# Merging small table and tail transfers, moving one decay to VectorE and two copies to ScalarE in a retention and two-MoE kernel

## The chip, the cores and the metric

One core of a Trainium2 chip runs the whole kernel. The metric is device time in microseconds, the median of several runs; one more execution is profiled and gives the trace. TensorE is called PE in the rows, VectorE DVE, ScalarE ACT, GpSimd POOL and SyncE SP. The cores' engines run side by side, each taking its own instructions in order, and wait for each other by semaphores.

## The reference

Three layers follow each other, in float32. `gamma` is one decay per head.

```
q, k, v: [4 batches, 8 heads, 576 tokens, 64]
scores = q @ k.T / 8 ;  ret = scores * gamma**(i - j) where i >= j, else 0
x = (ret @ v), heads side by side             -> [2304 tokens, 512]
h = x @ w_in ; g = h * sigmoid(1.702 h) ; x = g @ w_out          (2048 wide)
expert = argmax of cosine(x, expert_emb) / tau over 8 experts, gate = its softmax
out = gate * (relu(x @ w1[expert]) @ w2[expert])                 (1024 wide)
```

## The kernel before

The work is laid out by hand: every engine's instructions are emitted in a fixed order, and a float32 product is made of three products of a high and a low part. Four stages follow each other: attention (to about 71 us), the dense layers with the router beside them, the experts, and the last results. The change touches attention alone.

Attention works on "rows". A row is one batch and one pair of heads, so there are 16: rows 0 to 3 are batch 0, rows 4 to 7 batch 1, and so on. The first 512 of the 576 tokens are four chunks of 128; the 64 left over are the "ends" or "tails". A row comes in one transfer of 1024 KB (8 KB on each of 128 partitions): transposed keys, transposed queries, keys and values. The tails of a batch are a separate tensor, 768 bytes on each partition for each of four pairs. The decay tables are a third, 572 bytes on each partition and pair, after two masks that all pairs share. `load(bp)` issues the transfers that go with row `bp`, nearly all from SP's one queue, in the order in which they are called. Rows 0 to 8 are called for at the start, rows 9 to 15 when the slot of an earlier row is free. SP holds back an issue until the transfer eight issues earlier has landed, and PE's, VectorE's or GpSimd's reading of a slot when the slot is taken again.

Rows are computed in groups: [0], [1, 2], [3, 4], ... [13, 14], [15]. For a group `rows` with `nxt` and `then` the next two, the loop emits, in this order: GpSimd's decays for `then` (`decay_ends` scales the tails' queries of batches 2 and 3, `decay` the keys of a row, `decay_queries` the queries of batches 2 and 3); on PE the part of the output that comes from earlier chunks (`carried`) and the ends (`ends_out`), then `scores_end(nxt)`, the end products of the next group, then `scores` of the first row of `nxt`; on VectorE `masks` of that row (two instructions); then `values`, which interleaves on PE the chunks of `rows` with the four states of `nxt`. `state` multiplies decayed keys and values on PE, and ScalarE scales the result (L357). PE takes its instructions in order, so a late input of one holds up those behind it.

`DVE_ROWS` lists the rows whose `decay` VectorE does; all others are GpSimd's. For batches 0 and 1 an output row leaves PSUM by VectorE's multiplication (`keep`, L413). For batches 2 and 3 `keep` lets VectorE copy the odd rows (L409), and `kept_out` lets ScalarE copy those that are left (L419). The outputs have two banks of PSUM in turn, so row 15 takes the one that row 13 left.

From the group with row 11 on, a generator (`convert`) fills VectorE and ScalarE with the unpacking of the dense layers' weights: magnitude (ScalarE, L168), clamp and shift (VectorE, L181 and L183), two insertions (L191 and L196), high part (ScalarE, L171), low part (VectorE, L175). `flush` emits the pending magnitude or high part at the `yield`s. The dense layers begin with `layer1` (L576), the gate (ScalarE's tanh at L607, VectorE's product at L609) and `layer2` (L587).

Of the kernel before, what the change touches and what calls it, by code (L numbers as in the profile page):

```python
# [19 lines left out]
NPAIR = H // 2  # L20
# [26 lines left out]
STOP = 1000.0  # L47
EARLY = 5
WD_AT = (EARLY, 8, 9)
DVE_ROWS = (0, 2, 7, 8, 9)  # L50
NWD = 3
NBUF = 9
NBP = B * NPAIR
# [24 lines left out]
def retention_moe_kernel(  # L78
# [161 lines left out]
    def attention_(psum):  # L240
# [19 lines left out]
        def load(bp):  # L260
            t = row[bp]
            b, pair = divmod(bp, NPAIR)

            def load_tab(lo, hi):
                lo, hi = TX * (lo > 0) + TW * lo, TX + TW * hi
                SP.dma_start(tb[:, lo:hi], tab[:, lo:hi])

            def load_tails(lo, hi):
                SP.dma_start(tl[b][:, lo:hi], tails[b, :, lo:hi])

            if bp == 0:
                SP.dma_start(t[:, :AK], att[bp, :, :AK])
                ACT.dma_start(t[:, AK:], att[bp, :, AK:])
                load_tab(0, 1)
            if pair == 0:
                load_tails(0, 1 if b < 2 else NPAIR)
            if bp == 2:
                SP.dma_start(t[:, AK:], att[bp, :, AK:])
                load_tails(1, NPAIR)
                SP.dma_start(t[:, :AK], att[bp, :, :AK])  # L280
            elif bp:
                SP.dma_start(t, att[bp])
            if bp == 1:
                load_tab(1, 3)
            if bp == 2:
                load_tab(3, 4)
            if bp == 4:
                load_tails(1, NPAIR)

        load(0)  # L290
        DVE.memset(ones, 1.0)
# [11 lines left out]
        for bp in range(1, NBUF):  # L303
            load(bp)
# [19 lines left out]
        def masks(bp):  # L324
            pr = prs[bp % 3]
            for j in range(2):
                y, sc = (a.rearrange("p (c q) -> p c q", q=P) for a in (pr[:, 512 * j : 512 * (j + 1)], scs[j]))
                g = tbs[:, bp % NPAIR, TM + j : TM + j + 1]
                DVE.scalar_tensor_tensor(y, sc, g, tri.unsqueeze(1).to_broadcast(y.shape), ALU.mult, ALU.mult)  # L329

        def decay(bp):
            if bp < NBP:
                kd = row[bp][:, AK:AV].rearrange("p (c e) -> p c e", e=HD)
                dec = tbs[:, bp % NPAIR, TK:TS]
                (DVE if bp in DVE_ROWS else POOL).tensor_tensor(kd, kd, dec.unsqueeze(2).to_broadcast(kd.shape), ALU.mult)

        def decay_ends(bp):
            b, pair = divmod(bp, NPAIR)
            if b > 1 and pair == 0:
                qe = tl[b][:, :, TQ:TV]  # L340
                POOL.tensor_tensor(qe, qe, tbs[:, :, :TAIL], ALU.mult)

        def decay_queries(bp):
            b, pair = divmod(bp, NPAIR)
            if b > 1:
                qd = row[bp][:, AQ:AK].rearrange("p (c q) -> p c q", q=P)
                POOL.tensor_tensor(qd, qd, tbs[:, pair, :P].unsqueeze(1).to_broadcast(qd.shape), ALU.mult)

        def state(bp, ch):
            t = row[bp]  # L350
            if ch == 0:
                st["kv", bp] = psum.tile([P, 64], F32, tag="kv", bufs=2, name=f"s{bp}")
            s = st["kv", bp]
            for j, r in enumerate(heads):
                c0 = P * ch + 64 * j
                PE.matmul(s[r], t[:, AK + c0 : AK + c0 + 64], t[:, AV + c0 : AV + c0 + 64], start=ch == 0, stop=True, skip_group_check=ch > 0)  # L356
            ACT.activation(kvs[bp % 2][:, 64 * ch : 64 * ch + 64], s, AF.Copy, scale=tbs[:, bp % NPAIR, TS + ch : TS + ch + 1])  # L357
# [5 lines left out]
        def carried(bp):  # L363
            t, kv = row[bp], kvs[bp % 2]
            new_out(bp)
            for ch in range(1, NCH):
                for r in heads:
                    o = st["o", bp][r, P * ch : P * (ch + 1)]
                    first = ch == 1 and bp > 0
                    PE.matmul(o, kv[r, 64 * (ch - 1) : 64 * ch], t[r, AQ + P * ch : AQ + P * (ch + 1)], start=first, stop=True, skip_group_check=not first)  # L370
# [11 lines left out]
        def chunk(bp, ch):  # L382
            t, pr = row[bp], prs[bp % 3]
            for j, r in enumerate(heads):
                o = st["o", bp][r, P * ch : P * (ch + 1)]
                c0 = AV + P * ch + 64 * j
                first = bp + ch == 0
                PE.matmul(o, t[:, c0 : c0 + 64], pr[:, 512 * j + P * ch : 512 * j + P * (ch + 1)], start=first, stop=True, skip_group_check=not first)  # L388

        def kept_in(bp):  # L390
            b, pair = divmod(bp, NPAIR)
            if b > 1:
                tok = b * S - 2 * TB
                return x0f[pair][:, tok : tok + S]
            if ("x", bp) not in st:
                st["x", bp] = pool.tile([P, S], F32, tag="row", bufs=6, name=f"x{bp}")
            return st["x", bp]
# [7 lines left out]

        def keep(bp):
            if bp // NPAIR > 1:
                if bp % 2:
                    DVE.tensor_copy(kept_in(bp)[:, : NCH * P], st.pop(("o", bp)))  # L409
                return  # L410
            x, dec = kept_in(bp), tbs[:, bp % NPAIR, :P]
            y, o = (a.rearrange("p (c q) -> p c q", q=P) for a in (x[:, : NCH * P], st["o", bp]))
            DVE.tensor_tensor(y, o, dec.unsqueeze(1).to_broadcast(y.shape), ALU.mult)  # L413
# [26 lines left out]
        def values(rows, nxt):  # L440
            out = [(bp, ch) for bp in rows for ch in range(NCH)]
            at = [0, 3, 6, 8]
            for k, (bp, ch) in enumerate(out + [(None, None)]):
                if k in at and len(rows) + len(nxt) > 1:
                    for r in nxt:
                        state(r, at.index(k))
                if bp is not None:
                    chunk(bp, ch)
                if ch == NCH - 1:
                    keep(bp)  # L450
# [15 lines left out]
        for k, rows in enumerate(groups):  # L466
            nxt, then = (groups + [[], []])[k + 1 : k + 3]
            for bp in then:
                decay_ends(bp)
            for bp in then:  # L470
                if bp > 2 and bp not in DVE_ROWS:
                    decay(bp)
                decay_queries(bp)
            for bp in rows:
                carried(bp)
            ends_out(rows)
            if k:
                scores_end(nxt)
            for bp in rows:
                keep_end(bp)  # L480
            if k > 5:
                yield False
            if nxt:
                scores(nxt[0])
            if k == 0:
                decay(2)
                masks(nxt[0])
                keep(0)
                for ch in range(NCH):
                    for bp in nxt:  # L490
                        state(bp, ch)
                    if ch == 1:
                        scores(nxt[1])
                        masks(nxt[1])
                    else:
                        idle(4)
                scores_end(nxt)
            else:
                if nxt:
                    masks(nxt[0])  # L500
                values(rows, nxt)
            for bp in rows:
                if ("o", bp) in st:
                    kept_out(bp)
            make_lows(0 if k < 6 else 1)
            for bp in rows:
                if bp in WD_AT:
                    load_wd(WD_AT.index(bp))
                if bp in follows:
                    load(follows[bp])  # L510
                if follows.get(bp) == NBP - 1:

                    st["loaded"] = True
                    SP.dma_start(c[:, :CET], cst[:, :CET])
                    SP.dma_start(c[:, CET : CET + KD * E], embt)
                    uf = pool.tile([P, P], F32, tag="cvb", bufs=1, name="uf")
                    SP.dma_start(uf, cst[:, CU:CSL])
                    load_due()
            if k > 5:
                yield True  # L520
            for bp in nxt[1:] if k else []:
                scores(bp)
                masks(bp)
            for bp in then:
                if bp > 2 and bp in DVE_ROWS:
                    decay(bp)
            if 4 < k < 8:
                yield True
# [856 lines left out]
```

## Time and profile before

| | |
|---|---|
| median of 3 runs | 720.91 us (718.78 to 721.19) |
| profiled execution, its own time | 719.96 us |
| its span, first to last instruction | 718.1 us |
| PE busy | 702.8 us (98%) |
| PE weight load busy | 653.3 us (91%) |
| VectorE busy | 453.3 us (63%) |
| ScalarE busy | 306.6 us (43%) |
| GpSimd busy | 204.9 us (29%) |
| mean granted clock of TensorE | 0.995 of full speed |

The busy times are sums over the span. Matmuls are pipelined and their ends are modelled, so a row of PE can overlap the next one by some tenths of a microsecond, and a busy PE may hold short waits. The granted clock is the share of TensorE's full speed that the throttle let through.

### The profile page before, as it was taken

What the parts mean: (1) busy time and instruction counts of PE and PEld (TensorE: products, weight loads), DVE (VectorE), ACT (ScalarE), POOL (GpSimd) and SP (SyncE); (2) the same over time, 40 slices, a digit from 0 to 9 for tenths busy, and PEclk for the clock granted to TensorE, in tenths of its full rate; (3) what the DMA queues carried; (4) which work ended last, traced back from release to release, by engine and by line L of the source; (5) the groups of instructions that cost most, each with busy time, mean ns of one, the idle gap of its engine ahead of it and who ended that gap; (6) DMA issues with size and microseconds to landing.
All of it is one profiled execution on the core that took longest, in us unless ns stands there. A gap on an engine that the chain in (4) does not pass through costs nothing.

```text
span 718.1 us, 13166 instructions
## 1 busy us (share of the span) xinstructions
PE 702.8 (98%) x4903; PEld 653.3 (91%) x4903; DVE 453.3 (63%) x1036; ACT 306.6 (43%) x598; POOL 204.9 (29%) x193
## 2 busy tenths in 40 slices
PE   9999999999999999999999999999999999999995
PEld 7899789999989998998999899989999999998994
DVE  4678898888338886764475478555664464563551
ACT  3345454454273333322332253353454554554542
POOL 0773000000000240300120112323445656555563
PEclk9999999999999999999999999999999999999998
DMA  8999999000310040200300412235497979989761
GB/s 334 415 410 333 397 336 302 2 1 1 136 44 1 1 132 1 89 0 15 119 1 0 147 34 84 81 111 150 170 272 219 281 214 245 233 264 246 246 186 62
DMA packets 53156, 113.41 MB, mean 158 GB/s; under 512 B 8146, under 2 KB 29138, under 8 KB 48992
## 3 DMA queue, kind: packets, MB, share of 16 engines
q1 hardware_dynamic: 49744, 102.55, 44.8%
q0 software_dynamic: 3200, 9.46, 3.9%
q8 instruction: 39, 0.64, 0.4%
q10 hardware_dynamic: 144, 0.52, 0.2%
q14 instruction: 29, 0.24, 0.1%
HBM read 84.67 MB, written 28.17 MB: 157 GB/s over the span
## 4 chain that ended last, share of the span: by engine, by line
PE 82%; DMA 8%; DVE 3%; issue 3%; SPq 2%; ACT 1%; POOL 1%; POOLq 0%; ACTq 0%; DVEq 0%
PE o L587 28%; PE h L576 27%; PE eh L576 10%; PE eo L597 9%; DMA row<-att 3%; DMA we<-we 2%; PE ao L388 2%; PE sc L313 2%; DMA yd<-yq 1%; DMA y<-yd 1%; PE ao L370 1%; PE s L356 1%; SPq L836 1%; ACT unit L220 1%; DVE unit L221 1%
## 5 line engine op out<-in xcount | busy, mean ns | idle before, releaser
L576 PE MATMUL h<-x,unit 128*128 128x384 f32 x1152 | 217.5, 337 | 0.6 <-DVE g0t L609 0.6
L576 PEld LDWEIGHTS h<-x,unit 128*128 128x128 f32 x1152 | 204.6, 188 | 9.2 <-DVE g0t L609 0.9
L222 POOL TENSOR_TENSOR unit<-we,unit 128x512 fp32r<-128x512 f32 x64 | 103.1, 1619 | 120.8 <-ACT unit L220 102.8
L576 PE MATMUL eh<-xt,unit 128*128 128x336 f32 (+6 forms) x672 | 102.2, 301 | 0.7 <-DVE eg48l L621 0.6
L576 PEld LDWEIGHTS eh<-xt,unit 128*128 128x128 f32 x672 | 95.4, 188 | 1.5 <-DVE eg48l L621 0.8
L221 DVE TENSOR_TENSOR unit<-we,unit 128x512 fp32r<-128x512 f32 x64 | 53.6, 838 | 62.6 <-ACT unit L220 58.6
L220 ACT CAST unit<-we 128x1024 fp32r<-128x1024 f32 x64 | 66.8, 1046 | 26.9 <-DMA we<-we 24.7
L683 DVE CUSTOM_DVE_ANT_0 dj<-xr,en 128x512 bf16<-128x512 f32 x120 | 78.1, 698 | 0.0
L649 POOL TENSOR_TENSOR enrm<-scr,c 128x8 f32<-128x8 f32 x1 | 1.7, 1688 | 153.5 <-ACT ej L654 153.5
L626 POOL DMA_INDIRECT out<-y,idx x24 | 24.1, 1004 | 29.5 <-ACT y L849 19.2
L357 ACT ACTIVATE ends<-s,tb 128x64 f32<-128x64 f32 x64 | 17.4, 312 | 32.6 <-PE s L356 29.6
L626 POOL DMA_INDIRECT xs<-xr,slot x18 | 19.4, 1078 | 39.1 <-DVE xr L758 35.7
L743 POOL TENSOR_TENSOR cum<-cum,oh_all 128x8 bf16<-128x8 bf16 x18 | 4.8, 268 | 67.1 <-PE rk L736 52.4
L175 DVE TENSOR_TENSOR unit<-ca,unit 128x1024 fp32r<-128x1024 f32 x16 | 19.5, 1221 | 3.1 <-ACT unit L171 3.1
L549 POOL TENSOR_TENSOR x<-x0s,x 128x768 fp32r<-128x768 f32 x3 | 6.1, 2032 | 48.6 <-ACT x L548 48.6
L191 DVE SCALAR_TENSOR_TENSOR ca<-wd,ca 128x1024 int32<-128x1024 int32 x16 | 19.6, 1222 | 0.3
L196 DVE SCALAR_TENSOR_TENSOR ca<-wd,ca 128x1024 int32<-128x1024 int32 x16 | 19.5, 1219 | 0.1
L329 DVE SCALAR_TENSOR_TENSOR pr<-sc,tb 128x512 f32<-128x512 f32 x22 | 15.5, 745 | 5.9 <-PE sc L313 5.9
L849 ACT ACTIVATE y<-y,gate 128x512 f32<-128x512 f32 (+7 forms) x21 | 14.3, 713 | 11.1 <-DMA y<-yd 9.6
L313 PE MATMUL sc<-row 64*128 64x128 f32 x256 | 18.6, 285 | 0.3
L817 ACT CAST xt<-tp 128x336 fp32r<-128x336 f32 (+6 forms) x28 | 11.1, 411 | 18.2 <-DVE tp L815 18.2
L168 ACT ACTIVATE ca<-wd 128x1024 f32<-128x1024 f32 x16 | 18.4, 1152 | 0.0
(1311 smaller groups left out, 1531.7 us busy)
## 6 DMA issues: line engine op xcount, KB each, us to landing
we<-we SPq DMA_DIRECT2D x64, 512.0 KB
wd<-wd SPq DMA_DIRECT2D x16, 1024.0 KB
row<-att SPq DMA_DIRECT2D x14, 1024.0 KB
xs<-fill SPq DMA_DIRECT2D x22, 257.0 KB
xrow<-xr SPq DMA_DIRECT2D x18, 257.0 KB
y<-yd SPq DMA_DIRECT2D x7, 512.0 KB
x0d<-x0f SPq DMA_DIRECT2D x4, 768.0 KB
x0s<-x0d SPq DMA_DIRECT2D x8, 384.0 KB
```

The source lines that it names most:

```text
L175: DVE.tensor_tensor(units[u][:, 1, :], word(u).bitcast(F32), units[u][:, 0, :].bitcast(F32), ALU.subtract)
L191: DVE.scalar_tensor_tensor(a, d[:, :, 1], -0x40000000, a, ALU.bitwise_and, ALU.bitwise_or)
L196: DVE.scalar_tensor_tensor(a, d[:, :, 0], 29, a, ALU.logical_shift_right, ALU.bitwise_or)
L220: ACT.copy(w[:, 0, :], t)
L221: DVE.tensor_tensor(w[:, 1, :512], t[:, :512], w[:, 0, :512].bitcast(F32), ALU.subtract)
L222: POOL.tensor_tensor(w[:, 1, 512:], t[:, 512:], w[:, 0, 512:].bitcast(F32), ALU.subtract)
L313: PE.matmul(scs[j][:, P * ch : P * (ch + 1)], t[r, P * ch : P * (ch + 1)], t[r, AQ + P * ch : AQ + P * (ch + 1)], start=True, stop=True)
L576: PE.matmul(h, w[:, a, P * dc : P * (dc + 1)], xt[:, b, dc, :n], start=k == 0, stop=k == len(terms) - 1)
L587: PE.matmul(o, a[:, c0 : c0 + n], w[:, b, 512:], start=first and k == 0, stop=last and k == 2)
L597: PE.matmul(o, w[:, b, D + P * d : D + P * (d + 1)], a, start=first and k == 0, stop=last and k == 2)
L626: i = POOL.indirect_dma_start(out=dst[:, :], out_offset=bass.IndirectOffsetOnAxis(ap=rows, axis=0), in_=src, in_offset=None, bounds_check= ...
L683: DVE.tensor_tensor_reduce(junk, r[:, :D], en[e // 4][:, e % 4, :], 1.0, 0.0, ALU.mult, ALU.add, dots[:, E * k + e : E * k + e + 1])
```

## The change

Four things change, all in attention. The tables of pairs 1 to 3 come in one transfer instead of two (pairs 1 and 2, then 3). The tails of batch 1 come in one transfer, issued behind row 4, instead of one pair ahead of row 4 and three behind it; the tails of batches 2 and 3, which were one transfer each already, are issued behind the first row of their batch instead of ahead of it. VectorE decays row 4; its instruction stands in group [1, 2] behind the masks of row 3. VectorE no longer copies the outputs of rows 13 and 15, so `kept_out` has ScalarE copy them.

```diff
-DVE_ROWS = (0, 2, 7, 8, 9)
+DVE_ROWS = (0, 2, 4, 7, 8, 9)
...
-            if pair == 0:
-                load_tails(0, 1 if b < 2 else NPAIR)
+            if bp == 0:
+                load_tails(0, 1)
             if bp == 2:
                 SP.dma_start(t[:, AK:], att[bp, :, AK:])
                 load_tails(1, NPAIR)
                 SP.dma_start(t[:, :AK], att[bp, :, :AK])
             elif bp:
                 SP.dma_start(t, att[bp])
+            if b and pair == 0:
+                load_tails(0, NPAIR)
             if bp == 1:
-                load_tab(1, 3)
-            if bp == 2:
-                load_tab(3, 4)
-            if bp == 4:
-                load_tails(1, NPAIR)
+                load_tab(1, NPAIR)
...
         def keep(bp):
             if bp // NPAIR > 1:
-                if bp % 2:
+                if bp % 2 and bp < NBP - 3:
                     DVE.tensor_copy(kept_in(bp)[:, : NCH * P], st.pop(("o", bp)))
                 return
...
                 if nxt:
                     masks(nxt[0])
+                if k == 1:
+                    decay(4)
                 values(rows, nxt)
...
             for bp in then:
-                if bp > 2 and bp in DVE_ROWS:
+                if bp > 4 and bp in DVE_ROWS:
                     decay(bp)
```

## Rows read from the trace of the kernel before

**Rows 1.** Windows: stretch, its us, busy us (instructions) by engine, clock, DMA share, GB/s.
```profile
22.00:66.00 44.00, 44.00 (x858) 40.75 (x854) 31.78 (x56) 22.55 (x74) 30.20 (x32) 1.00 0.98 388
...
70.80:90.00 19.20, 17.65 (x88) 15.51 (x89) 15.78 (x22) 8.90 (x15) 0.00 (x0) 1.00 1.02 395
```

**Rows 2.** Waits of PE: us in total, times, longest us.
```profile
PE s L356 <- POOL row L335: 1.2, 1, 1.2
...
PE o L587 <- DVE g1l L614: 0.6, 1, 0.6
PE h L576 <- DVE g0t L609: 0.6, 1, 0.6
```

**Rows 3.** Chain that ends last, 5 to 26 us: start, us, what.
```profile
9.15 11.45 DMA row<-att
...
20.68 1.05 POOL row L335
```

**Rows 4.** DMA rate by window; SP's issue of row 9 (start, us); SP's waits.
```profile
20.00:21.00 1.00, 0.53 (x10) 0.27 (x6) 0.70 (x2) 0.31 (x1) 0.33 (x1) 1.00 1.08 436
...
18.32 0.35 SPq L282 DMA_DIRECT2D row<-att  x1
...
SPq L282 <- DMA ends<-tails: 0.4, 1, 0.4
```

**Rows 5.** Timeline, 18 to 22 us: start, us, engine, line, operation, out<-in [idle before].
```profile
18.77 0.40 PE L319 MATMUL sct<-ends 64*64 64x64 f32 x8
...
20.30 1.41 DVE L329 SCALAR_TENSOR_TENSOR pr<-sc,tb 128x512 f32<-128x512 f32 x2 [0.34 <-PE sc L313]
...
21.77 0.34 PE L356 MATMUL s<-row 128*64 128x64 f32 x4 [1.24 <-POOL row L335]
```

**Rows 6.** Decays (L335): VectorE's durations (ns, min/median/max), then three in the timeline.
```profile
L335 DVE TENSOR_TENSOR row<-row,tb x5: 681/693/1417, 6.3 to 42.0; 128x512 f32<-128x512 f32 x5
...
24.05 1.05 POOL L335 TENSOR_TENSOR row<-row,tb 128x512 f32<-128x512 f32 x1 [0.82 <-DMA row<-att]
...
41.86 1.05 POOL L335 TENSOR_TENSOR row<-row,tb 128x512 f32<-128x512 f32 x1
...
42.04 1.42 DVE L335 TENSOR_TENSOR row<-row,tb 128x512 f32<-128x512 f32 x1
```

**Rows 7.** PE's warm-up in the timeline; windows about the last matmul.
```profile
1.06 4.62 PE L299 MATMUL warm<-ones 128*128 128x128 bf16 x46 [1.06 <-DVE ones L291]
...
709.00:710.00 1.00, 0.55 (x3) 0.26 (x3) 0.54 (x1) 0.99 (x3) 0.00 (x0) 1.00 0.02 8
...
711.00:712.00 1.00, 0.00 (x0) 0.00 (x0) 0.00 (x0) 0.00 (x0) 0.70 (x2) 0.79 0.18 70
712.00:713.00 1.00, 0.00 (x0) 0.00 (x0) 0.00 (x0) 0.00 (x0) 0.69 (x2) 0.50 0.51 193
```

**Rows 8.** GpSimd's timeline about row 8; the chain at the end products of rows 7, 8.
```profile
30.55 0.70 POOL L341 TENSOR_TENSOR more<-more,tb 128x256 f32<-128x256 f32 x1
32.49 1.27 POOL L347 TENSOR_TENSOR row<-row,tb 128x512 f32<-128x512 f32 x1 [1.23 <-DMA row<-att]
...
35.20 0.23 PE sct L319 x8
```

**Rows 9.** Timeline at the end of attention.
```profile
68.65 0.87 PE L370 MATMUL ao<-row,ends 64*64 64x128 f32 x12
...
69.04 0.58 ACT L419 COPY x0f<-ao 128x512 f32<-128x512 f32 x1
...
69.68 1.09 PE L388 MATMUL ao<-pr,row 128*64 128x128 f32 x16
...
69.91 1.18 ACT L168 ACTIVATE ca<-wd 128x1024 f32<-128x1024 f32 x1
...
72.70 0.69 DVE L181 TENSOR_SCALAR ca<-ca 128x1024 f32<-128x1024 f32 x1
...
75.17 0.55 DVE L609 SCALAR_TENSOR_TENSOR g0t<-g0t,h 128x384 f32<-128x384 f32 x1
```

## The prediction

> **What bounds the kernel now.** I read the busy time by stage first. In the 44 us from 22 to 66 us the reader is to see TensorE busy for 44.00 us, with VectorE at 31.78 and GpSimd at 30.20; from 70.8 to 90 it is busy for 17.65 of 19.20 us [rows 1]. So a microsecond that TensorE loses inside attention is never won back, and an edit to another engine can pay only through one of TensorE's few waits. The list of waits names the ones in reach [rows 2]: one of 1.2 us for GpSimd's decay of row 4, and 0.6 and 0.6 us for VectorE where the dense layers begin. The chain that ends last shows the first of them: row 4 lands at 20.61, GpSimd decays it in 1.05 us, and only then does TensorE start that row's state [rows 3]. Together these waits hold about 2.4 us, the most that the change could give back.
>
> **The change part by part.**
>
> *Pieces of tables and tails in one transfer.* SP's queue is first in, first out, and row 4 now goes ahead of all tails of batch 1. Before, the first pair's piece of them (96 KB by its shape, 768 bytes on 128 partitions) went ahead of row 4, the other three behind it. The old first piece had landed by 18.32, when SP, which had waited for it, issued its next row [rows 4]; TensorE multiplied the ends of rows 3 and 4 at 18.77 and did not wait [rows 5]. Now row 4 lands at 20.61 less 96 KB / 436 GB/s = 0.23, so at 20.4 (the rate is that of the microsecond before the landing), and the tails of batch 1, 384 KB by their shape, follow at about that rate 0.9 us later, at 21.3. (SP issues two transfers fewer before them, some 0.4 us each, but it waits for landings, not the other way round: nothing.) They are one transfer, so the end product of row 4 needs all of it, and TensorE's queue holds the scores of row 3 behind that product. This is the wait that is added: 21.3 - 18.77 = 2.5 us. What is queued behind it: the scores of row 3, VectorE's masks on them, and now the decay of row 4.
>
> *VectorE decays row 4.* GpSimd took 1.05 us from 20.68 [rows 3]; VectorE takes 0.69 when alone (its median) [rows 6]. But in VectorE's queue the decay stands behind both masks of row 3, which began 20.30 - 18.77 = 1.53 us after the end product and took 1.41 us [rows 5]. From 21.3 that gives 22.85 and 24.25. Meanwhile GpSimd, rid of row 4, takes row 5 when it lands, at 24.05 before [rows 6], now about 0.1 sooner, and decays it until 25.0. Two such decays side by side are in the trace once: GpSimd's ran from 41.86 to 42.91 at its usual length, and VectorE's, begun at 42.04, took 1.42 us and ended 0.55 after it [rows 6]. The same here ends row 4's decay at 25.55; alone it would be 24.95. TensorE's state of row 4 then starts at 25.6 instead of 21.77 [rows 5]: **+3.8 us** (alone +3.2), the 2.5 us of the tails included. Bounds: 0.7 if the tails did not wait at all (masks end at 21.71, decay at 22.4), 4.5 if the decay also ran 0.7 late. I take 3.8, because tails, row 5 and masks all hang on the same queue and move together.
>
> *TensorE's clock.* Before state 4 TensorE would stand idle twice, for about 2.4 us and, after the scores and one state, for about 2.7 us. At the end of the trace it last worked for 0.55 us of the slice from 709 to 710, and the granted clock falls in the slice from 711 to 712, whose mean is 0.79 (it stands at 0.50 after), some 2 us later [rows 7]: the lower of its two levels, 1.2 GHz. I take it that one of the two idle stretches does this. At the start of the program the kernel lets TensorE run 46 small matmuls for 4.62 us before any work [rows 7]. Bounds: nothing, if the clock stays up; 4.62 / 2 = 2.3 us, if it needs as long to come back and every matmul takes twice its time meanwhile. I take **+1.6 us**, nearer the upper end, since from 22 us on TensorE's time is all matmuls [rows 1].
>
> The Trainium skill (TensorE: Matmul & The Clock Gate, "Why this matters for your kernels") counsels only against idle gaps somewhat longer than these two; by it this term would be nothing and the sum 4.6 us. The trace's own fall came after a shorter stretch, so I keep the term.
>
> *Tables of three pairs at once.* The bytes are the same; the half row 2 now stands behind 71.5 KB more, 0.2 us at 436 GB/s, which can delay the masks of row 1 by as much. It is covered: TensorE waits for the tails until 21.3 either way. Without that wait it would cost 0.2.
>
> The Trainium skill (DMA: Bandwidth & Descriptors, "Bandwidth") calls transfers of up to 64 KB descriptor-dominated, 138 GB/s against 341 for 1 MB; estimated by that page the 96 KB take 0.7 us, and merging would bring the tails 0.5 us nearer. Here SP waited 0.4 us for that piece [rows 4], so I credit nothing more.
>
> *Tails of batches 2 and 3 behind their first row.* Row 8 landed at about 32.47, when GpSimd began on its queries; the tails of batch 2 now land there instead, the row 0.9 earlier. GpSimd's 0.70 us on these tails ends at about 33.2, and TensorE reads them at 35.20, later still after the shift [rows 8]: nothing. If that cover were gone, it would be those 0.9 us.
>
> *ScalarE copies rows 13 and 15.* VectorE loses two copies of 0.69 us. Row 13's bank is the one row 15's output takes next (two banks in turn), so TensorE's carried product of row 15, at 68.65, now waits for ScalarE, whose first copy of the pair starts at 69.04, behind the last scaled state of row 15, and ends at 69.62 [rows 9]: +0.95. Row 15's own copy then stands in ScalarE's queue before the magnitude of the next dense weights: matmuls of row 15 end at 70.77 + 0.95 = 71.7, copy 0.58, magnitude 1.18, so 73.5 instead of 71.09. VectorE, which without its copies could go on earlier, needs it for its clamp: 73.5 instead of 72.70 [rows 9], and the gate of the first block, at 75.17, moves with it. TensorE waited 0.6 us for that gate [rows 2], so it resumes 0.8 later than before: **+0.8 us**. Bounds: +0.3 (0.95 less the 0.6 returned), +0.95.
>
> **Sum.** 3.8 + 1.6 + 0.8 = +6.2 us, on the profiled execution's own 719.96 us: 726.2. The median of the runs, 720.91, is 0.95 higher, inside their spread of 2.4, so I leave it there.
>
> **The rivals.**
> 1. *The clock stays up.* For it: both idle stretches are broken by 1.6 us of matmuls. Against: [rows 7]. 719.96 + 4.6 = 724.6.
> 2. *The tails are in time* (some queue brings them before 18.8), and only masks before the decay and the exit cost: 0.7 + 0.8 = 1.5, 721.5. Against: one queue in order, rows 3 and 4 landing 2.7 us apart.
> 3. *Faster: row 4's landing is all that mattered.* Row 4 at 20.4, decay in 0.69 ahead of the masks, state at 21.1, -0.7; and VectorE, relieved of 1.4 us at the exit, lets both waits of 0.6 go: -1.2. 718.1. It decides if the end product does not wait for the tails and the decay is not held behind the masks; the order of both queues speaks against it.
> 4. *Worse:* the clock falls in both stretches or the exit's waits add to a second fall, +9: 729.
> That the transfers are not merged at all is excluded by their code.
>
> **How the numbers follow.** Chances: forecast 0.42, clock up 0.30, tails in time 0.14, faster 0.06, worse 0.08. The forecast's own range is 724.5 to 728; down to the case without tails and up to the worse one the range is 721.3 to 728.8. About 0.3%, 2.2 us, is what a measurement of this kernel can tell from no change: forecast, clock up and worse are slower (0.80); tails in time is the same (0.15, with a little of the others); faster 0.05.
>
> **What would show it.** After: TensorE's first of the two end products at about 18.8 and the scores of row 3 not before 21; a wait of TensorE for a tails transfer; VectorE's decay of row 4 after the masks and over 1 us long; state 4 near 25.6; a granted clock under 1.00 in the slices between 21 and 30; TensorE waiting for ScalarE's copy before row 15's carried product; the first gate 0.8 us later than before, counted from the last state of row 15. State 4 before 22.5 would make the forecast wrong.

## The result, and the profile of the changed kernel

The changed kernel takes 725.99 us (median of 5 runs, 725.48 to 726.59), the kernel before 720.14 beside it (5 runs, 718.67 to 721.19): the ratio is 1.0081 with a 95% interval of 1.0066 to 1.0096, some 5.9 us more. The profiled execution took 726.16, over a span of 724.3; that of before took 719.96 over 718.1, so 6.2 us lie between the two profiles.

The stage first. The windows of the changed kernel, with the columns of [rows 1]:

```profile
22.00:66.00 44.00, 40.26 (x729) 37.30 (x726) 29.04 (x52) 18.12 (x62) 27.43 (x30) 0.92 0.88 340
...
24.00:25.00 1.00, 0.00 (x0) 0.00 (x0) 1.00 (x1) 0.00 (x0) 0.72 (x1) 0.58 1.06 442
26.00:27.00 1.00, 1.00 (x16) 1.00 (x14) 0.00 (x0) 0.23 (x1) 0.84 (x1) 0.50 1.03 426
30.00:31.00 1.00, 1.00 (x14) 0.88 (x12) 0.69 (x1) 0.61 (x3) 0.00 (x0) 0.51 1.01 417
31.00:32.00 1.00, 1.00 (x20) 0.88 (x18) 0.13 (x1) 1.00 (x4) 0.60 (x1) 1.00 1.04 431
```

Two things differ from [rows 1]. TensorE stands idle for 3.74 of the 44 us in which it had no idle time, and its granted clock is not 1.00 throughout: it is at half, 1.2 GHz, from 24.2 to 31.0 us (the two ends are worked out from the means 0.58 and 0.51 of their windows).

TensorE's waits in the changed kernel (us in total, times, longest), to be read beside [rows 2]:

```profile
PE s L354 <- DVE row L333: 2.6, 1, 2.6
PE sct L317 <- DMA ends<-tails: 1.2, 1, 1.2
PE s L354 <- issue: 1.1, 1, 1.1
PE ao L368 <- ACT x0f L417: 0.9, 1, 0.9
...
PE h L576 <- DVE g0t L609: 0.4, 1, 0.4
```

Four waits are new, and the 1.2 us for GpSimd that the change took away is not among them any more. In the timeline of the changed kernel (start, us, engine, line, operation, [idle before]) they stand in this order; its lines answer to [rows 5, 6 and 9]:

```profile
19.50 0.28 PE L317 MATMUL sct<-ends 64*64 64x64 f32 x4
21.03 0.33 PE L317 MATMUL sct<-ends 64*64 64x64 f32 x4 [1.24 <-DMA ends<-tails]
22.48 1.41 DVE L327 SCALAR_TENSOR_TENSOR pr<-sc,tb 128x512 f32<-128x512 f32 x2 [0.34 <-PE sc L311]
23.68 1.04 POOL L333 TENSOR_TENSOR row<-row,tb 128x512 f32<-128x512 f32 x1 [3.54 <-DMA row<-att]
23.81 1.46 DVE L333 TENSOR_TENSOR row<-row,tb 128x512 f32<-128x512 f32 x1
25.32 0.48 PE L354 MATMUL s<-row 128*64 128x64 f32 x4 [2.60 <-DVE row L333]
33.59 0.40 PE L317 MATMUL sct<-ends 64*64 64x64 f32 x8
39.05 1.55 POOL L436 TENSOR_TENSOR x<-x,x 128x384 fp32r<-128x384 f32 x2 [2.71 <-ACT x L426]
40.56 1.30 POOL L345 TENSOR_TENSOR row<-row,tb 128x512 f32<-128x512 f32 x1
40.60 3.26 DVE L333 TENSOR_TENSOR row<-row,tb 128x512 f32<-128x512 f32 x2
41.80 1.51 POOL L333 TENSOR_TENSOR row<-row,tb 128x512 f32<-128x512 f32 x1
43.27 1.54 POOL L345 TENSOR_TENSOR row<-row,tb 128x512 f32<-128x512 f32 x1
43.96 0.34 PE L354 MATMUL s<-row 128*64 128x64 f32 x4 [1.07 <-issue]
76.41 1.06 ACT L417 COPY x0f<-ao 128x512 f32<-128x512 f32 x2
77.04 0.87 PE L368 MATMUL ao<-row,ends 64*64 64x128 f32 x12 [0.95 <-ACT x0f L417]
79.21 0.59 ACT L417 COPY x0f<-ao 128x512 f32<-128x512 f32 x1 [0.81 <-PE ao L386]
79.69 1.13 ACT L168 ACTIVATE ca<-wd 128x1024 f32<-128x1024 f32 x1
80.86 0.69 DVE L181 TENSOR_SCALAR ca<-ca 128x1024 f32<-128x1024 f32 x1 [1.91 <-ACT ca L168]
83.33 0.55 DVE L609 SCALAR_TENSOR_TENSOR g0t<-g0t,h 128x384 f32<-128x384 f32 x1
83.93 2.37 PE L576 MATMUL h<-x,unit 128*128 128x384 f32 x12 [0.40 <-DVE g0t L609]
```

The reader follows how far the changed kernel lies behind at each landmark. State 4 starts at 25.32, against 21.77 in [rows 5]: 3.55 late. The next end products start at 33.59, where before they start at 27.63: 5.96 late, so 2.4 were lost under the low clock. They are still 5.97 late at the following pair (41.00 against 35.03), but the scores of row 8 (46.89 against 39.52) are 7.37 late: the 1.4 between them lies at TensorE's wait ahead of the state of row 8, of which its row counts 1.07 as idle. The third group of matmuls of the first dense block, behind the gate, starts at 83.93, in the kernel before at 75.77: 8.16 late, 0.8 more. From there to the end 1.9 us come back (below).

The wait of 1.07 has "issue" for its releaser, so its cause has to be read from VectorE: its two decays of rows 7 and 8 take 3.26 us together. The same stretch in the timeline of the kernel before:

```profile
34.64 1.68 DVE L335 TENSOR_TENSOR row<-row,tb 128x512 f32<-128x512 f32 x2
...
34.68 1.08 POOL L438 TENSOR_TENSOR x<-x,x 128x192 fp32r<-128x192 f32 x1
...
35.23 1.08 DVE L335 TENSOR_TENSOR row<-row,tb 128x512 f32<-128x512 f32 x1
...
35.73 1.74 POOL L347 TENSOR_TENSOR row<-row,tb 128x512 f32<-128x512 f32 x1
```

The two decays of the changed kernel one by one:

```profile
40.60 1.81 DVE L333 TENSOR_TENSOR row<-row,tb 128x512 f32<-128x512 f32 x1
...
42.33 1.53 DVE L333 TENSOR_TENSOR row<-row,tb 128x512 f32<-128x512 f32 x1
```

GpSimd works beside the pair in both kernels; what differs is who begins first. In the kernel before, VectorE's first decay begins 0.04 us ahead of a GpSimd instruction and is through when the second begins at 35.23; GpSimd's takes 1.08 instead of 0.59 (its length at 19.55 in the changed kernel, with VectorE idle), and only the second decay is long, 1.08. In the changed kernel GpSimd begins 0.04 ahead, both decays are long, 1.81 and 1.53, and GpSimd's next two instructions take 1.51 and 1.54, where they take 1.05 and 1.09 undisturbed.

### The profile page after: what moved, and what is told of

The parts are those of the page before. It is cut to its first block, busy times and chain, and to the rows that moved or that the text cites. A ratio compares the mean times of both kernels' runs of the same rounds, so it can differ in the third digit from the quotient of the medians.

```text
span 724.3 us, 13166 instructions
## 1 busy us (share of the span) xinstructions
PE 706.3 (98%) x4903; PEld 657.0 (91%) x4903; DVE 458.1 (63%) x1035; ACT 308.1 (43%) x600; POOL 202.3 (28%) x192
## 5 line engine op out<-in xcount | busy, mean ns | idle before, releaser
L221 DVE TENSOR_TENSOR unit<-we,unit 128x512 fp32r<-128x512 f32 x64 | 57.5, 898 | 59.9 <-ACT unit L220 58.2
L354 PE MATMUL s<-row 128*64 128x64 f32 x256 | 16.7, 244 | 4.3 <-DVE row L333 2.6
L327 DVE SCALAR_TENSOR_TENSOR pr<-sc,tb 128x512 f32<-128x512 f32 x22 | 15.5, 745 | 7.6 <-PE sc L311 7.6
L354 PEld LDWEIGHTS s<-row 128*64 128x64 f32 x256 | 13.0, 145 | 7.7 <-DVE row L333 2.7
```

The source lines that it names most:

```text
L221: DVE.tensor_tensor(w[:, 1, :512], t[:, :512], w[:, 0, :512].bitcast(F32), ALU.subtract)
```

## Experiments

Each kernel was timed beside the kernel before on the same chip, and its ratio is against that; "profile" is its one profiled execution.

**Both kernels once more, unchanged.** They tell what repeats.

> The kernel before, unchanged, for a second profile. In its first profile TensorE waited 1.0 and 0.6 us in the experts, which the changed kernel's profile did not show, and the stretch from the first expert matmul to the last transposed result took 221.3 us against 219.4. If that difference is chance, this profile may draw anything from 219.4 to 221.5; if the change removed those waits, it draws about 221.3 again. Granted clock at 1.00 throughout attention by every theory.

> The changed kernel, unchanged, for a second profile. Theory A: half clock again for some 6 us behind state 4, VectorE's decays of rows 7 and 8 again over 3 us together beside GpSimd, TensorE waiting about 0.9 us for ScalarE's copy of row 13. The experts' stretch anything from 219.4 to 221.5 us if its difference is chance, about 219.4 if it belongs to the change.

Measured: 718.34 and 726.67 us. The four waits, the pair of decays (3.27 us, GpSimd again 0.04 ahead) and the low clock (22 to 32 us: 0.66 in both executions of the changed kernel) come again; the wait for the tails is 1.79 instead of 1.24, and state 4 starts at 25.28. The group behind the gate starts at 83.51 against 75.57: 7.94 late. What does not repeat is what I took for a gain. From the first matmul of the experts to their last transposed result it was 221.32 us in the first profile of before, 219.42 in the first of after: 1.9 in favour of the change. The second pair has 220.01 and 220.30, and the profiles of the other kernels from 219.02 to 221.57, without order. So those 1.9 us are a difference of two executions, and no effect of the change.

**The first tails early again.** Of the changed kernel, only the order of the transfers ahead of row 4 is put back:

```diff
-            if bp == 0:
+            if bp == 0 or bp == 4:
                 load_tails(0, 1)
...
-                load_tails(0, NPAIR)
+                load_tails(1 if b == 1 else 0, NPAIR)
```

> Batch 1's first pair of tails goes ahead of row 4 again, the other three behind it; all else as changed. Theory A (tails late, masks ahead of the decay, GpSimd's decay in its way, two idle stretches, then the clock at half): without the tails' wait TensorE has one idle stretch of about 2 us, VectorE decays row 4 at 21.7 to 22.4 with GpSimd idle, state 4 starts near 22.5 instead of 25.3, the clock stays at 1.00 and the time falls to 721.6 (0.8 of the exit and 0.7 of state 4 over the 720.1 of before). Rival B (the late tails are the whole loss): 720.1 to 720.9. Rival C (the decay on VectorE is the whole loss): no change, 726.

Measured: 723.03 us (8 runs), ratio 1.0057 (1.0033 to 1.0080). In its timeline:

```profile
21.71 0.68 DVE L333 TENSOR_TENSOR row<-row,tb 128x512 f32<-128x512 f32 x1
22.45 0.34 PE L354 MATMUL s<-row 128*64 128x64 f32 x4 [1.83 <-DVE row L333]
```

No wait for tails is left, the decay is alone and takes 0.68, the clock is 1.00 from 22 to 66 us and the pair of rows 7 and 8 takes 1.68. State 4 is 0.7 later than before, which is the lower bound of the prediction's term. The times decide less: the profiled 720.48 is 1.1 under theory A's 721.6 and inside rival B's range, the median is above both. What speaks against B is the trace, in which state 4 is still 0.7 late and TensorE still waits 0.9 for ScalarE's copy. The times lie in two groups, four from 720.48 to 722.24 and four from 723.82 to 726.60 (the next kernel, too, has three of ten from 723.30 on). No profile shows the second group. The mean granted clock of the executions is 0.997, 0.997, 0.996 and 0.994 in the first group and 0.995, 0.994, 0.997 and 0.992 in the second: a fall of the clock after the idle stretch may be part of 726.60, but the 724.54 at 0.997 lost its time in another way, which stays open.

**GpSimd decays row 4 again.** Of the changed kernel, only that:

```diff
-DVE_ROWS = (0, 2, 4, 7, 8, 9)
+DVE_ROWS = (0, 2, 7, 8, 9)
...
-                if k == 1:
-                    decay(4)
```

> GpSimd decays row 4 as before, ahead of row 5; tails and all else as changed. Theory A: the tails' wait stays (scores of row 3 at about 21.3), but state 4 starts right behind state 3 at about 22.5, so there is one idle stretch of TensorE, the clock stays at 1.00, and the time is 721.6. Rival B (late tails are the whole loss): stays at 725.5 to 726.5. Rival C: 720.1 to 720.9.

Measured: 721.27 us (10 runs), ratio 1.0035 (1.0015 to 1.0054). In its timeline:

```profile
21.00 0.33 PE L317 MATMUL sct<-ends 64*64 64x64 f32 x4 [1.74 <-DMA ends<-tails]
22.35 0.45 PE L354 MATMUL s<-row 128*64 128x64 f32 x8
```

The wait for the tails is there in full, but behind it the states of rows 3 and 4 go in one run at 22.35, and the clock from 22 to 32 us is 1.00. The next states start at 23.29 instead of 22.59: in this profile the tails alone cost 0.7, since the old wait of 1.24 for GpSimd [rows 5] lay in the same place, and they replace it rather than add to it. Only with the decay behind the masks does the delay grow to 3.55. Rival B, which put nearly all of the loss on the tails, falls, and so does C, which put all of it on the decay: without that decay 0.15% or more is left.

**The decay ahead of the masks.** Of the changed kernel, the two lines in the other order:

```diff
+                if k == 1:
+                    decay(4)
                 if nxt:
                     masks(nxt[0])
-                if k == 1:
-                    decay(4)
```

> VectorE's decay of row 4 stands ahead of the masks of row 3 instead of behind them; all else as changed. Theory A: it runs behind the two small products on the tails, at about 22.1 to 22.8, with GpSimd idle, so it takes 0.69 us and not 1.46; state 4 starts at about 22.9, the second idle stretch is gone, the clock stays at 1.00; 722.0. Rival B (late tails are the whole loss): 725.5 to 726.5, since they are as late as before.

Measured: 722.35 us (5 runs), ratio 1.0046 (1.0028 to 1.0064). In its timeline:

```profile
22.43 0.68 DVE L333 TENSOR_TENSOR row<-row,tb 128x512 f32<-128x512 f32 x1
22.74 0.76 PE L354 MATMUL s<-row 128*64 128x64 f32 x8
```

The decay takes 0.68, state 4 follows state 3 without a pause, and the clock from 22 to 32 us is 1.00. But this profile does not test the late tails: TensorE came to the end products only at 21.33, and the tails were there. It had lost its time earlier (the second and third line are windows):

```profile
15.55 1.48 PE L311 MATMUL sc<-row 64*128 64x128 f32 x16 [1.37 <-DMA row<-att]
...
16.00:17.00 1.00, 1.00 (x16) 0.78 (x12) 0.00 (x0) 0.00 (x0) 0.00 (x0) 0.62 1.05 442
...
19.00:20.00 1.00, 1.00 (x19) 1.00 (x20) 0.30 (x2) 0.68 (x3) 0.49 (x1) 0.67 1.04 430
```

It waited 1.37 us for row 2, and the clock was at half from 16.2 to 19.7 us, so the 722.35 holds a loss from there. Theory A, by which the clock stays up once the second idle stretch is gone, does not hold: here one stretch of 1.37 us was enough, while in the kernel with the transfers alone one of 1.47 us at the same place left it at 1.00. The pair of rows 7 and 8 took 3.26 us here with TensorE waiting 1.1: that collision does not need the low clock.

**Matmuls into the idle stretches.** The changed kernel, and TensorE multiplies a constant into a part of a tile that nobody reads, 18 times ahead of row 4's end product and 40 times ahead of its state:

```diff
+        def busy(n):
+            for _ in range(n):
+                PE.matmul(sct[:64, 256:384], ones[:, :64], ones, start=True, stop=True)
...
+                if bp == 4:
+                    busy(18)
...
+                        if r == 4 and k == 0:
+                            busy(40)
```

> TensorE gets small matmuls on constant data, whose result nobody reads, where it idled: 18 ahead of row 4's end product and 40 ahead of state 4; all else as changed. Theory A: state 4 still starts at about 25.3, but the granted clock stays at 1.00, and what the clock cost between state 4 and the ends of rows 3 and 4 (about 2.4 us) comes back: 723.6. Rival D (the slow stretch behind state 4 is not the clock's, but that of waits on other engines): 726.

Measured: 724.38 us (4 runs), ratio 1.0070 (1.0049 to 1.0092). Its timeline, then its windows:

```profile
22.98 2.40 PE L315 MATMUL sct<-ones 128*64 128x128 bf16 x40
25.39 0.34 PE L360 MATMUL s<-row 128*64 128x64 f32 x4
...
31.24 0.40 PE L323 MATMUL sct<-ends 64*64 64x64 f32 x8
```

```profile
22.00:32.00 10.00, 9.98 (x190) 9.29 (x190) 6.10 (x13) 3.50 (x12) 4.80 (x6) 1.00 1.01 415
...
32.00:66.00 34.00, 32.82 (x636) 30.27 (x632) 25.86 (x44) 15.53 (x54) 22.69 (x25) 1.00 0.86 334
```

State 4 starts no earlier than in the changed kernel, but the clock is 1.00, and the end products follow after 5.85 us (kernel before: 5.86, from 21.77 to 27.63), not after 8.27 or, in the second profile of the changed kernel, 7.88. This gives the clock's term: 2.0 to 2.4 us. That the idle time of TensorE brings it is borne out by the next kernel, which has these matmuls too and 1.00 from 22 to 66 us; the three profiles with the same late transfers and late decay but no such matmuls (two of the changed kernel, one of the kernel with VectorE's copies below) all have a low clock there. The medians alone would not: the interval of this ratio overlaps that of the change. In the second window 1.18 us are idle, almost all of it the collision, which stays.

**The same, with the decays of rows 7 and 8 earlier.** Added to the last kernel:

```diff
+                if k == 2:
+                    decay(7)
+                    decay(8)
...
-                if bp > 4 and bp in DVE_ROWS:
+                if bp > 8 and bp in DVE_ROWS:
```

> As the kernel with fillers (ratio 1.0070), and VectorE decays rows 7 and 8 right behind the masks of row 5, where GpSimd has no work, instead of behind the masks of row 6. Theory A2 (the two engines' decays lock each other out, and the late start of state 4 moved them on top of each other): the pair takes 1.4 us instead of 3.26, TensorE's wait of 1.1 us ahead of row 8's state is gone, 1.4 us less, ratio about 1.0050. Rival F (the wait comes from another cause, such as row 8's landing): 1.0070 and the wait stays.

Measured: 722.74 us (8 runs), ratio 1.0045 (1.0025 to 1.0066). Its timeline, then its windows:

```profile
34.24 1.29 DVE L339 TENSOR_TENSOR row<-row,tb 128x512 f32<-128x512 f32 x2
```

```profile
32.00:66.00 34.00, 34.00 (x664) 31.47 (x664) 24.86 (x47) 16.57 (x59) 21.87 (x25) 1.00 0.88 340
```

Away from GpSimd's work the pair takes 1.29 us, and TensorE has no idle time left in the stretch where it had 1.18. So the collision is a cost of its own, which neither the late transfers nor the clock make up: both are as in the kernel with matmuls added.

**VectorE copies rows 13 and 15 again.** Of the changed kernel, only that:

```diff
-                if bp % 2 and bp < NBP - 3:
+                if bp % 2:
```

> VectorE copies rows 13 and 15 again; all else as changed. Theory A: the wait of 0.9 us ahead of row 15's carried product is gone, the magnitude comes 0.8 us earlier; 0.8 us less than the changed kernel, ratio to before about 1.0070 where the changed one has 1.0081. Rival E (the copies on ScalarE cost nothing, since VectorE is the bound at the start of the dense layers): 1.0081 or more.

Measured: 724.33 us (5 runs), ratio 1.0075 (1.0049 to 1.0101), which covers both expectations. The trace settles it: TensorE's wait for ScalarE's copy is gone, and that for the gate is 0.6 again, as in [rows 2], instead of 0.4. It shows one thing more, in a line of its timeline and a window:

```profile
21.14 0.33 PE L317 MATMUL sct<-ends 64*64 64x64 f32 x4 [2.11 <-DMA ends<-tails]
...
21.00:22.00 1.00, 0.85 (x10) 0.79 (x12) 0.47 (x3) 0.00 (x0) 0.00 (x0) 0.78 1.10 442
```

Here the clock fell at about 21.6, after the wait for the tails alone and before the one for the decay.

**Each part by itself, on the kernel before.** The transfers only; VectorE's decay of row 4 behind the masks only; ScalarE's two copies only (the edits are the hunks of the change).

> The kernel before with the transfers of the change alone; GpSimd decays row 4, VectorE copies rows 13 and 15. Theory A: TensorE waits some 2 us for the tails of batch 1, but state 4 follows state 3 at about 22.4, 0.7 us later than before, with one idle stretch; ratio 1.001 to 1.002, with a few executions up to 1.005 where that one stretch costs the clock. Rival B (late tails are the whole loss): 1.007 to 1.008.

> The kernel before with VectorE's decay of row 4 behind the masks of row 3 alone; transfers and copies as before. Theory A: the decay runs at about 21.7 to 22.4 in 0.69 us, GpSimd having nothing at hand, and state 4 starts 0.7 us later than before; one idle stretch of about 2 us; ratio 1.001, up to 1.005 in executions that lose the clock. Rival C (the decay's place is the whole loss): 1.007 to 1.008.

> The kernel before with ScalarE's copies of rows 13 and 15 alone. Theory A: TensorE waits 0.9 us ahead of row 15's carried product, and the first gate comes 0.8 us later; ratio 1.001. Rival E (the relief of VectorE pays): 0.998 to 1.000. If the three parts alone add up to about 2.2 us (1.003) and the whole change to 5.8, the rest belongs to their meeting: the clock and the two engines' decays.

Measured: 1.0021 (1.0008 to 1.0035), 1.0020 (1.0006 to 1.0035) and 1.0012 (0.9998 to 1.0027); 10 runs each. Together 0.53%, 3.8 us, against 5.9 for the whole. The 2 us between them are within what these intervals leave open, but the traces show what they can be. In the window from 22 to 32 us the clock of all three is 1.00, where the changed kernel has 0.66. The pair of rows 7 and 8 takes 2.54, 2.37 and 2.72 us in them, between the 1.68 of before and the 3.26 of the change. The 2.72 is in the kernel whose code differs from before only in the copies, far behind that place: the collision depends on how the two engines happen to stand to each other. In the five profiles with 3.26 or 3.27 GpSimd's multiplication begins 0.03 to 0.04 us ahead of VectorE's pair; where VectorE is ahead, or GpSimd further on, the pair takes less (1.68 in the first-tails kernel, in spite of its delay).

With the transfers only, TensorE also waited 1.47 us at 15.5 us for row 2, as in the two kernels above with 1.37 (decay ahead of the masks) and 1.32 (matmuls added). Three of the nine profiles with the new transfers have this wait, none of the five with the old ones; that is too few to say that the merged tables, which now stand ahead of half of row 2, bring it.

**The parts that paid, in the right order.** The kernel before with VectorE's decay of row 4 *ahead* of the masks, and with row 15's copy, and that alone, on ScalarE, *behind* the magnitude of the dense weights; all transfers as before:

```diff
-DVE_ROWS = (0, 2, 7, 8, 9)
+DVE_ROWS = (0, 2, 4, 7, 8, 9)
...
-                if bp % 2:
+                if bp % 2 and bp < NBP - 1:
...
+                if k == 1:
+                    decay(4)
                 if nxt:
                     masks(nxt[0])
...
-                if ("o", bp) in st:
+                if ("o", bp) in st and bp < NBP - 1:
...
+            if k == 8:
+                kept_out(NBP - 1)
```

> The kernel before with VectorE's decay of row 4 ahead of the masks of row 3, and ScalarE's copy of row 15 alone, behind the pending magnitude; row 13's copy stays on VectorE, the transfers are as before. Theory A: state 4 starts 0.4 us earlier, at about 21.4, and VectorE reaches the first gate 0.6 us earlier; 1.0 us less than before, ratio 0.9985. Rival: the waits only move, 1.000.

Measured: 717.65 us (12 runs) against 719.11 (34 runs), ratio 0.9979 (0.9967 to 0.9990): faster than both kernels, by 1.5 us against the kernel before. Its timeline:

```profile
20.53 0.69 DVE L335 TENSOR_TENSOR row<-row,tb 128x512 f32<-128x512 f32 x1 [0.40 <-DMA row<-att]
21.28 0.34 PE L356 MATMUL s<-row 128*64 128x64 f32 x4 [0.57 <-DVE row L335]
69.45 1.19 ACT L168 ACTIVATE ca<-wd 128x1024 f32<-128x1024 f32 x1
70.52 0.59 ACT L419 COPY x0f<-ao 128x512 f32<-128x512 f32 x1
74.10 0.54 DVE L613 SCALAR_TENSOR_TENSOR g0t<-g0t,h 128x384 f32<-128x384 f32 x1
```

State 4 waits 0.57 instead of 1.24, and the gate comes at 74.10, early enough that TensorE does not wait for it (0.6 in [rows 2]). So row 4's decay on VectorE and row 15's copy on ScalarE pay together, at other places in the two queues; the merged transfers are not in this kernel.

## Why the prediction was right

The forecast of 726.2 us is the profiled 726.16 and, within 0.2, the median. The case that I chose is the one that took place, but its terms came out otherwise, one was missing, and so close an agreement is partly luck.

1. *Tails and decay, +3.8: measured +3.55.* The tails were there at 21.03 (forecast 21.3), the decay stood behind the masks and took 1.46 us beside GpSimd's 1.04 (the 1.42 of the one pair in [rows 6]), and state 4 started at 25.32 (forecast 25.6). TensorE waited only 1.24 for the tails instead of 2.5, since its first end product was itself late in this execution, at 19.50 against 18.77 in [rows 5]; in the second it waited 1.79. It is the landing that sets the sum, not the length of the wait. The price of the two parts was not separable as the prediction put it ("the 2.5 us of the tails included"): in their profiles the tails without the decay cost 0.7 at this point, the decay with the first tails in time 0.7 as well, and both together 3.5.
2. *Clock, +1.6: measured 2.0 to 2.4.* That TensorE's idle time would bring the clock down was right and the term too small; the upper bound of 2.3, taken from the 4.62 us of warm-up in [rows 7] at half speed, was the better estimate. The low clock lasted 6.8 us. The Trainium skill (TensorE: Matmul & The Clock Gate, "Why this matters for your kernels") counsels against idle gaps longer than the two of this case; here the clock fell some 1.4 us into the second one, and in two other kernels after a single one of 1.37 and of 2.11 us, so the measurement decides against it as a safe limit. That two stretches together do it is not shown: single ones of 1.47, 1.74 and 1.83 us left the clock at 1.00 in their profiles, and what decides stays open.
3. *The collision of rows 7 and 8, +1.4: not foreseen.* The prediction weighed VectorE beside GpSimd for row 4, and then took the later decays as they were, although everything behind state 4 was to move by 5 us while GpSimd's queue takes its time from other releasers. [Rows 6] shows the same kind of decay at 0.69 alone and 1.42 beside GpSimd; two of them at the wrong moment could have been priced at 2 x 0.73 = 1.5, estimated from that row. Whether it would come to that hung on a lead of 0.04 us of GpSimd's instruction, which no row of the kernel before could tell.
4. *Exit, +0.8: measured +0.8.* The carried product waited 0.95 for ScalarE (forecast 0.95), and the gate's wait shrank from 0.63 to 0.40. Shown again from the other side by the kernel with VectorE's copies, which has neither.
5. *What the prediction held at nothing.* The tables in one transfer and the tails of batches 2 and 3 behind their row: no wait of TensorE for either is in the list of waits of the changed kernel's two profiles. That held there; in three other profiles with these transfers TensorE waited 1.3 to 1.5 us for row 2, which the prediction did not have, and whose cause is not shown.
6. *The sum.* 3.55 + 2.41 + 1.40 + 0.80 = 8.16, as measured behind the gate, and 8.16 - 1.9 = 6.26, within 0.1 of the 6.2 between the first two profiles. The terms that I left out or made too small are 2.2 us; the experts' stretch, which has nothing to do with the change, gave 1.9 back in this pair. In the second pair nothing came back: 7.94 behind the gate, 8.33 at the end. The medians are 5.9 apart (4.8 to 6.9 by the interval of the ratio), less than either pair shows lost up to the first gate. The 720.14 of the kernel before lies above its medians beside the experiments (719.49, 719.33 and 719.11), and the second profile's 726.67 is 7.3 above the 719.33 beside it, so 5.9 may be low. Whether executions without a profile lose less to clock and collision, or four profiles are too few for that stretch, was not settled.

Rival 1 (clock up, 724.6) is near what the kernel with added matmuls measured, 724.38, though that has the collision in it; rival 2 (tails in time, 721.5) lies between the profiled 720.48 and the median 723.03 of the kernel with the first tails early, whose trace has both of its terms. Rival 3's idea, row 4 decayed ahead of the masks and the exit relieved, was not the change but is in part the last kernel, 1.5 us below the kernel before where the rival had 1.9, and without its earlier landing of row 4.

## What to carry to other kernels

A small transfer that somebody waits for is not to be merged with a large one behind it, and an operation moved to a faster engine is to be priced with its place in that engine's queue: the decay of 0.69 us shortened TensorE's wait from 1.24 to 0.57 ahead of the masks, and behind them and behind late tails it made state 4 3.55 late. An idle stretch of TensorE of 1.4 us can bring a fall of the clock, which cost another 2 us here, in some executions and not in others, so one profile with the clock up does not clear a wait. After a delay is forecast, go on down the timeline and ask which engines do not move with it, because whatever they then run beside each other has a new price; and take a second profile of both kernels before adding up terms of a microsecond.

## What the runs showed of the hardware

- VectorE's decays and GpSimd's multiplications and subtractions of two tensors in SBUF hold each other up, and in these traces the one that begins first runs at its usual length. VectorE's pair of decays takes 1.29 us without GpSimd, 1.68 or 2.37 where it begins 0.01 to 0.07 us ahead of a GpSimd instruction, and 3.26 where GpSimd's begins 0.04 ahead; GpSimd's next instructions then take 1.51 and 1.54 instead of 1.05 and 1.09. The Trainium skill (SBUF — State Buffer, "Who interferes with whom") says that such an instruction of VectorE contends with one of GpSimd that reads SBUF, by an exclusive lock; the alternation in the trace agrees.
- After short idle stretches of TensorE the clock went to 0.50 and stayed there for 6.8 us (24.2 to 31.0), although TensorE was busy again from 25.32 on. It did so after one stretch of 1.37 us (low for 3.4 us) and one of 2.11 us too, and not after others of 1.32 to 1.83 us. With small matmuls on a constant in the idle time it was 1.00 from 22 to 66 us in both kernels that had them.
- A stretch of the same work takes 219.0 to 221.6 us from execution to execution.
